# Top-32 attention before two dense layers on one core: early first products of chunk 0, values prepared in three steps, chunk 3 starting chunk 4, and x's two forms in one buffer

## The chip, the core and the metric

The program runs on one core of a Trainium2 chip. The metric is the device time of one execution in microseconds. The engines are PE (TensorE; PEld is its weight loads), DVE (VectorE), ACT (ScalarE), POOL (GpSimd) and SP, which issues the DMAs. Each takes its instructions in one fixed order.

## The reference

Attention for 4 batches of 8 heads, 576 rows of 64, in which each row keeps its 32 largest scores, and then two dense layers over the 2304 x 512 result (`scale` is 1/8):

```python
scores = scale * np.matmul(q, k.transpose(0, 1, 3, 2))
kth = np.partition(scores, -32, axis=-1)[..., -32:-31]
scores = np.where(scores >= kth, scores, -1000000000.0)
attn = softmax(scores)
x = np.matmul(attn, v)          # then heads side by side: 2304 x 512
x = (sigmoid(x @ w_gate) * (x @ w_val)) @ w_out      # 512 -> 1536 -> 512
x = np.maximum(x @ w_in, 0.0) ** 2 @ w_out2           # 512 -> 2048 -> 512
```

## The kernel before

The 2304 rows are 18 blocks of 128. `CHUNKS` groups them into 12 chunks: chunks 0 to 5 are one block each (N = 128), chunks 6 to 11 are two (N = 256). The attention of a chunk runs over four pairs of heads (`Pair`); a **unit** is one head and one block. A unit is scores on PE (`sp`), a copy to SBUF on ACT, seven ranking steps on DVE (`rank`: max, match_replace, max, ... so k = 0 to 6), the softmax on ACT and POOL, a transpose, and, once per pair, the product with the values (`xp`), copied by ACT into x of the chunk.

Chunks 0 and 1 (`PLAIN`) run their two layers in fp32 (`moe32`): products `pg` of six pairs of feature blocks (`fp`), tanh on ACT (`th`), the sum `acc1`, copied by ACT into `x_plain` again, then `ph` and `acc2`. While they run, ACT, DVE and POOL turn the weights, which arrive as 64-bit words, into fp32 (`conv`, ACT's lines L613 and L620). Later chunks use fp16 pairs (high and low part) in `moe`: `pg`, `pv` (layer 1), `acc1`, then `x2` with a common scale (a sum of squares by a product with ones, `x2pq`, and a maximum on DVE), then `ph`, `acc2`. `split_x` makes the two fp16 parts of x for chunks 2 to 5; ACT squares them first (`x_5pq` is the sum for chunk 5).

From chunk 4 on (`PRE0`), a chunk computes `NPRE` = 2 pairs of the next chunk's layer 1 ahead (`nxt`, into the tile `gp`), the first before its own last `acc1`, the others between `x2`'s squares and its second layer. Chunk 3 does not.

The attention of chunks 6 to 11 takes its values in fp16 pairs from DRAM. They are prepared once per batch and pair of heads, 12 times: `prep_values` loads the fp32 values (`vm`, `ve`), ACT squares them with a running sum (L204) and copies the sums to bf16 (L208); `split_values` sums over partitions on PE (`vn`, L217), DVE makes a power of two of it, ACT and POOL make the two parts (`vom`, `voe`; `vom` is in the tag `vo`, which has one buffer), and SP writes them out (`vd`).

Tiles of a tag share its buffers: `m4` has three of 4 KB per partition (x, its fp16 parts, `gp`, an early x2 and others), `acc` two PSUM banks, `wk` two, `tr` two.

The order on each engine is settled when the program is built: a scheduler takes the instructions by priority (`at`, `tc.high_priority`) and dependence. The main loop hands it attention units, weight steps and layer steps by due times `ta`, `tw`, `tm`; later, `lead` says how many units attention is ahead of the layers.

Of the kernel before, what the change touches and what calls it, by code (L numbers as in the profile page):

```python
# [21 lines left out]
P = 128  # L22
# [18 lines left out]
PRE0 = 4  # L41
# [6 lines left out]
SM2 = ()  # L48
# [18 lines left out]
KA = 7  # L67
GLATE = 30.0
EARLY = ("wg", "wv")
PB = 10  # L70

# [5 lines left out]
def tile_topk_attention__then__two_moe_layers(  # L77
# [111 lines left out]
    def prep_values(b, hp):  # L189
# [8 lines left out]
        for r in range(2):  # L198
            nc.sync.dma_start(ve[r * ST : (r + 1) * ST], src[:, SM:S].rearrange("h p d -> p h d"))
        om = apool.tile([P, 2, 2, CB, D], F16, tag="vo", bufs=1, name=f"vom_{n}")  # L200
        oe = apool.tile([P, 2, 2, D], F16, tag="we", bufs=3, name=f"voe_{n}")
        sm = apool.tile([P, 8], F32, tag="bs", bufs=3, name=f"vs_{n}")
        for x, (o, t) in enumerate(((om, vm), (oe, ve))):
            nc.scalar.activation(  # L204
                o[:, :, 0].bitcast(BF16), t, AF.Square, accum_out=sm[:, x : x + 1]
            )
        sb = sm.bitcast(BF16)[:, 4:6]
        nc.scalar.copy(sb, sm[:, 0:2])  # L208
        late_values.append((b, hp, n, vm, ve, om, oe, sm))

    late_values = []
# [77 lines left out]
    class Pair:  # L289
# [9 lines left out]
        def load(self):  # L299
            ci, hp = self.ci, self.hp  # L300
            for tt in self.tts:
                qn = apool.tile([P, 2, 2, D], F32, tag="qn", bufs=2, name=f"qn_{tt}_{hp}")
                for b, s0, o, n in pieces(tt):
                    for a in range(2):
                        nc.sync.dma_start(
                            qn[o : o + n, :, a, :],
                            q[b, 2 * hp : 2 * hp + 2, s0 : s0 + n].rearrange("h p d -> p h d"),
                        )
# [27 lines left out]
        def queries(self, tts):  # L336
            for tt in tts:
                qn = self.qt[tt]
                pt = ps_t.tile([P, 512], F32, tag="tr", name=f"qpt_{tt}_{self.hp}")
# [129 lines left out]
        def transpose(self, j, i, wk, dg):  # L469
# [7 lines left out]
            tp = ps_t.tile([P, 512], F32, tag="tr", name=f"tp_{tt}_{h}")  # L477
# [444 lines left out]
    def moe32(ci, xt):  # L922
# [4 lines left out]
        def l1_pair(fp):  # L927
            pg = ps_w.tile([P, 512], F32, tag="wk", name=f"pg_{ci}_{fp}")
            for t, name in enumerate(("wg", "wv")):
                for e in range(2):  # L930
                    for c in range(KM):
# [4 lines left out]
                            start=(t == 0 and e == 0 and c == 0),  # L936
                            stop=(c == KM - 1),
                            skip_group_check=True,
                        )
            th = mpool.tile([P, 2 * N], F32, tag="hi", bufs=HIB, name=f"th_{ci}_{fp}")  # L940
# [21 lines left out]

        prev = None
# [59 lines left out]
    done = set()  # L1023
    xsp = {}
# [6 lines left out]
    def attention():  # L1031
# [62 lines left out]
        def tail(n, after=None):  # L1094
# [30 lines left out]
            if j == 1 and i == len(pr.tts) - 1:  # L1125
                if pr.ci < TCI:
                    pr.values()
                if pr.hp == NHP - 1:
# [38 lines left out]
        for n in range(last + 1):  # L1167
# [8 lines left out]
            for u, k in orders(n):  # L1176
                if u in state:
# [9 lines left out]
                    seq.append(ins)  # L1187
            turns()
# [3 lines left out]
            while ci >= TCI - 2 and late_values:  # L1192
                split_values(*late_values.pop(0), seq[-1])
# [64 lines left out]
    for ci in PLAIN:  # L1258
        n = 0
        while True:  # L1260
            if nstep[0] == len(steps):
                tw = 1e8
            if body is None and ci in xsp:
                have("wv")
                body = moe32(ci, xsp.pop(ci))
# [88 lines left out]
```

## Time and profile before

| | |
|---|---|
| median of three runs | 1227.74 us (1220.72, 1227.74, 2309.37) |
| the profiled execution | 1218.28 us |
| its span, first to last instruction | 1216.2 us |
| PE busy, idle | 1158.1 us, 58.1 us |
| mean granted clock of PE | 0.989 |

The last of the three runs was disturbed as a whole; the other two and the profiled execution lie within 9.5 us. 2.08 us of the profiled execution lie outside its span.

### The profile page before, as it was taken

What the parts mean: (1) busy time and instruction counts of PE and PEld (TensorE: products, weight loads), DVE (VectorE), ACT (ScalarE), POOL (GpSimd) and SP (SyncE); (2) the same over time, 40 slices, a digit from 0 to 9 for tenths busy, and PEclk for the clock granted to TensorE, in tenths of its full rate; (3) what the DMA queues carried; (4) which work ended last, traced back from release to release, by engine and by line L of the source; (5) the groups of instructions that cost most, each with busy time, mean ns of one, the idle gap of its engine ahead of it and who ended that gap; (6) DMA issues with size and microseconds to landing.
All of it is one profiled execution on the core that took longest, in us unless ns stands there. A gap on an engine that the chain in (4) does not pass through costs nothing.

```text
span 1216.2 us, 30575 instructions
## 1 busy us (share of the span) xinstructions
PE 1158.1 (95%) x11477; PEld 941.4 (77%) x11477; DVE 919.5 (76%) x1921; ACT 802.0 (66%) x1695; POOL 833.4 (69%) x1294
## 2 busy tenths in 40 slices
PE   6879999999799799999999999999999999999998
PEld 5659878878679678788787688768876886886875
DVE  5899878899779988999999799999699969010010
ACT  3999985777767777777778667766577666222122
POOL 1698984687875688878879967896597659324223
PEclk9889999999899999999999999999999999999999
DMA  6999963324353477666676666556245513200000
GB/s 153 355 359 320 305 181 105 89 68 133 99 148 104 116 153 156 143 138 135 144 173 136 137 146 130 122 117 145 50 89 126 99 40 63 45 1 1 18 1 18
DMA packets 243187, 153.91 MB, mean 127 GB/s; under 512 B 193120, under 2 KB 209504, under 8 KB 243040
## 3 DMA queue, kind: packets, MB, share of 16 engines
q1 hardware_dynamic: 243040, 151.97, 49.3%
q8 instruction: 90, 1.47, 0.5%
q14 instruction: 57, 0.47, 0.1%
HBM read 105.51 MB, written 18.09 MB: 102 GB/s over the span
## 4 chain that ended last, share of the span: by engine, by line
PE 48%; DVE 2%; DMA 1%; SPq 0%; issue 0%; ACT 0%; POOL 0%; DVEq 0%; POOLq 0%
PE acc L899 10%; PE ph L878 10%; PE acc L813 7%; PE pv L773 7%; PE pg L773 7%; PE sp L381 3%; PE xp L516 3%; DVE mx L392 1%; DVE W L393 1%; PE qpt L341 1%; DMA kn<-in_k_dram 1%; DMA PT<-pp 0%; PE kpt L167 0%; PE x2pq L845 0%; DVE x2s L848 0%
## 5 line engine op out<-in xcount | busy, mean ns | idle before, releaser
L392 DVE MAX8 mx<-W 128x8 f32<-128x576 f32 x432 | 327.7, 759 | 10.9
L393 DVE MATCH_REPLACE8 W<-mx,W 128x576 f32<-128x576 f32 x288 | 213.9, 743 | 0.0
L878 PE MATMUL ph<-x,wi_w 128*128 128x256 f16 (+1 forms) x1920 | 191.8, 252 | 4.4 <-ACT r L887 2.8
L899 PE MATMUL acc<-w_w,rh 128*128 128x512 f16 x768 | 182.2, 379 | 1.6 <-POOL rh L891 1.6
L878 PEld LDWEIGHTS <-wi_w 128*128 128x128 f16 x1920 | 155.9, 98 | 30.7 <-issue 4.7
L773 PE MATMUL pg<-xs,wg_w 128*128 128x256 f16 (+1 forms) x1440 | 145.4, 251 | 1.3 <-ACT th L783 1.3
L773 PE MATMUL pv<-xs,wv_w 128*128 128x256 f16 (+1 forms) x1440 | 142.6, 251 | 2.1 <-DVE x2s L848 1.7
L381 PE MATMUL sp<-kst,qt 128*128 128x288 f32 x608 | 132.9, 328 | 9.4 <-DMA kst<-ks 4.7
L464 POOL TENSOR_TENSOR pp<-S,pp 128x512 f16<-128x512 f32 x192 | 137.1, 736 | 1.9
L773 PEld LDWEIGHTS <-wg_w 128*128 128x128 f16 x1440 | 117.2, 98 | 19.1 <-issue 3.4
L418 ACT ACTIVATE S<-S,mx 128x576 f32<-128x576 f32 x144 | 111.8, 776 | 27.7 <-DVE mx L392 27.3
L813 PEld LDWEIGHTS <-wo_w 128*128 128x128 f16 x1440 | 118.7, 99 | 13.9 <-issue 2.4
L899 PEld LDWEIGHTS <-rh 128*128 128x128 f16 x768 | 72.1, 98 | 73.4 <-POOL rh L891 1.8
L773 PEld LDWEIGHTS <-wv_w 128*128 128x128 f16 x1440 | 117.0, 98 | 15.4 <-issue 2.7
L392 DVE MAX8 mx<-S 128x8 f32<-128x576 f32 x144 | 107.2, 745 | 26.6 <-ACT S L384 26.4
L384 ACT COPY S<-sp 128x576 f32<-128x576 f32 x144 | 91.8, 637 | 50.6 <-PE sp L381 44.9
L785 DVE TENSOR_TENSOR th<-pv,th 128x512 f32<-128x512 f32 (+1 forms) x60 | 34.6, 576 | 119.2 <-PE pv L773 118.5
L462 POOL TENSOR_SCALAR S<-S,bs 128x576 f32<-128x576 f32 x96 | 71.9, 749 | 54.4 <-ACT pp L461 53.7
L393 DVE MATCH_REPLACE8 W<-mx,S 128x576 f32<-128x576 f32 x144 | 106.9, 743 | 0.0
L813 PE MATMUL acc<-gh,wo_w 128*128 128x256 f16 (+1 forms) x1104 | 104.9, 249 | 1.9 <-ACT gh L788 1.9
L381 PEld LDWEIGHTS sp<-kst,qt 128*128 128x128 f32 x608 | 90.2, 191 | 18.9 <-DMA kst<-ks 5.0
L890 POOL TENSOR_TENSOR r<-r 128x512 f32<-128x512 f32 (+1 forms) x80 | 69.5, 871 | 48.5 <-ACT rh L889 47.4
(236 smaller groups left out, 2222.2 us busy)
## 6 DMA issues: line engine op xcount, KB each, us to landing
kst<-ks SPq DMA_DIRECT2D x112, 288.0 KB, 3.1
v<-vd SPq DMA_DIRECT2D x32, 320.0 KB, 3.5
qn<-in_q_dram SPq DMA_DIRECT2D x128, 64.0 KB, 2.5
wi_r<-in_moe_w_in_dram SPq DMA_DIRECT2D x16, 512.0 KB, 6.4
w_r<-in_moe_w_out_dram SPq DMA_DIRECT2D x16, 512.0 KB, 4.9
v<-in_v_dram SPq DMA_DIRECT2D x56, 128.0 KB, 2.4
wg_r<-in_moe_w_gate_dram SPq DMA_DIRECT2D x12, 512.0 KB, 6.1
wv_r<-in_moe_w_val_dram SPq DMA_DIRECT2D x12, 512.0 KB, 7.3
```

What stands on the lines that cost most here:

```text
L381: nc.tensor.matmul(sp[:, e, 0:HALF], l, r, start=(x == 0), stop=(x == len(ops) - 1))
L384: nc.scalar.copy(ss.rearrange("p (e s) -> p e s", e=2), sp[:, :, 0:HALF])
L392: return nc.vector.max(m8, st.cur).ins
L393: ins = nc.vector.match_replace(st.wk, m8, st.cur, NEG).ins
L418: nc.scalar.activation(wk, wk, AF.Prelu, bias=kth, scale=-1.0, alpha=1.0 / BIG)
L462: nc.gpsimd.tensor_scalar(wk, wk, rz, 1.0, op0=ALU.mult, op1=ALU.mult)
L464: nc.gpsimd.tensor_tensor(pp[:, o : o + e - f], wk[:, f:e], pp[:, f:e], op=ALU.subtract)
L773: nc.tensor.matmul(pp[:, e * N : (e + 1) * N], wblk(wd, a, c, f0, P), xs[:, b_, c, :], start=(e == 0 and n == 0), stop=(n == 3 * KM - 1), ...
L813: nc.tensor.matmul(accs[d // 2][:, (d % 2) * N : (d % 2 + 1) * N], wblk("wo", a, f, d * P, P), gh[:, b_, e * N : (e + 1) * N], start=(f == ...
L878: nc.tensor.matmul(ph[:, e * N : (e + 1) * N], wblk("wi", a, c, f0, P), x2[:, b_, c, :], start=(e == 0 and n == 0), stop=(n == 3 * KM - 1) ...
L890: nc.gpsimd.tensor_tensor(r, r, r, op=ALU.mult)
L899: nc.tensor.matmul(acc2[i][:, 0:DM], gh[:, b_, e * N + i * P : e * N + (i + 1) * P], wblk("w2", a, f, 0, DM), start=(f == 0 and x == 0), s ...
```

## The change

- `products` takes the columns (`cs`) of x that a step works on. For chunk 0, once three of its four pairs of heads are in x, a first step of `moe32` issues the products of `FIRST` = 2 pairs `fp` with the first `XC` = 3 quarters of x; `l1_pair` then adds the fourth quarter alone.
- `QACC` = 2: the query transposes of chunk 0's first two pairs of heads go to a bank of `acc`, not `tr`. (`SIDEQ` and `TACC` are 0 and do nothing.)
- `prep_values` loads only. The squares and the copy (`norm_values`) are issued in the ranking of a unit, after its step k = 4 (`KB`), and `split_values` after step k = 6 (`KC`). The sums `sm` get a buffer of their own; they used the softmax's tag `bs`.
- `PRE0` = 3: chunk 3 too computes two pairs of the next chunk's layer 1 ahead, and its attention lead is `LEAD2` = 14 units, not `LEAD` = 10.
- `SM2`: for chunks 2 to 5 the fp16 parts of x lie in the second half of x's own buffer, not in a second buffer of `m4`.

```diff
-PRE0 = 4
+PRE0 = 3
...
-SM2 = ()
+SM2 = (2, 3, 4, 5)
...
+QACC = 2
...
+KB = 4
+KC = 6
+FIRST = 2
+FUP = 0
+XC = 3
...
+        later.append((KB, norm_values, (b, hp, n, vm, ve)))
+
+    later = []
+
+    def norm_values(b, hp, n, vm, ve, after):
         om = apool.tile([P, 2, 2, CB, D], F16, tag="vo", bufs=1, name=f"vom_{n}")
         oe = apool.tile([P, 2, 2, D], F16, tag="we", bufs=3, name=f"voe_{n}")
-        sm = apool.tile([P, 8], F32, tag="bs", bufs=3, name=f"vs_{n}")
+        sm = apool.tile([P, 8], F32, tag="sm", bufs=1, name=f"vs_{n}")
         for x, (o, t) in enumerate(((om, vm), (oe, ve))):
-            nc.scalar.activation(
+            sq = nc.scalar.activation(
                 o[:, :, 0].bitcast(BF16), t, AF.Square, accum_out=sm[:, x : x + 1]
             )
+            tc.add_manual_dep(sq.ins, after.name, NOSYNC, reason="loaded by then")
         sb = sm.bitcast(BF16)[:, 4:6]
         nc.scalar.copy(sb, sm[:, 0:2])
-        late_values.append((b, hp, n, vm, ve, om, oe, sm))
-
-    late_values = []
+        later.append((KC, split_values, (b, hp, n, vm, ve, om, oe, sm)))
...
-                pt = ps_t.tile([P, 512], F32, tag="tr", name=f"qpt_{tt}_{self.hp}")
+                pool, tag = (ps_a, "acc") if self.ci == 0 and self.hp < QACC else (ps_t, "tr")
+                pt = pool.tile([P, 512], F32, tag=tag, name=f"qpt_{tt}_{self.hp}")
...
-        def l1_pair(fp):
-            pg = ps_w.tile([P, 512], F32, tag="wk", name=f"pg_{ci}_{fp}")
+        early = {}
+
+        def products(fp, cs):
+            fresh = fp not in early
+            if fresh:
+                early[fp] = ps_w.tile([P, 512], F32, tag="wk", name=f"pg_{ci}_{fp}")
+            pg = early[fp]
             for t, name in enumerate(("wg", "wv")):
                 for e in range(2):
-                    for c in range(KM):
+                    for c in cs:
...
-                            start=(t == 0 and e == 0 and c == 0),
+                            start=(fresh and t == 0 and e == 0 and c == cs[0]),
...
+        def l1_pair(fp):
+            products(fp, range(XC if fp in early else 0, KM))
+            pg = early.pop(fp)
...
+        if ci == PLAIN[0] and FIRST:
+            for fp in range(FIRST):
+                products(fp, range(XC))
+            yield
...
                     seq.append(ins)
+                    while later and later[0][0] == k:
+                        _, fn, args = later.pop(0)
+                        fn(*args, ins)
...
-            while ci >= TCI - 2 and late_values:
-                split_values(*late_values.pop(0), seq[-1])
...
+            if (
+                ci == PLAIN[0]
+                and FIRST
+                and body is None
+                and xdone.get(ci, 0) >= XC
+                and nstep[0] > NF1 // 2 + XC // 2
+            ):
+                body = moe32(ci, xts[ci])
+                at(max(ta, tw) - FUP)
+                next(body)
+                tm = 1e9
```

**How the order changes.** On PE, just after x of chunk 0 is complete (`tp_1_0` is a transpose for the next chunk, `pg_0_0` the first product pair, `x_plain` x, `wg_c`, `wv_c` the weights), before:

```order
L665 MATMUL wv_n_590<-wv_d_793,ones_86 128x128
L482 MATMUL tp_1_0_1079<-dg_1_0_1014,S_1_0_822 128x128 x4
L932 MATMUL pg_0_0_1040<-x_plain_335,wg_c1_280 128x128
L932 MATMUL pg_0_0_1040<-x_plain_335,wg_c0_209 128x128 x2
L932 MATMUL pg_0_0_1040<-x_plain_335,wg_c1_280 128x128 x2
L932 MATMUL pg_0_0_1040<-x_plain_335,wv_c0_524 128x128
L381 MATMUL sp_1_4_1163<-kst_1_4_0_1062,qt_1_2_0_1074 128x288
L932 MATMUL pg_0_0_1040<-x_plain_335,wv_c0_524 128x128
```

and now, one pair of heads earlier, right behind `tp_0_6`:

```order
L496 MATMUL tp_0_6_935<-dg_0_6_866,S_0_6_627 128x128 x4
L951 MATMUL pg_0_0_868<-x_plain_335,wg_c1_280 128x128
L951 MATMUL pg_0_0_868<-x_plain_335,wg_c0_209 128x128 x2
L951 MATMUL pg_0_0_868<-x_plain_335,wg_c1_280 128x128
L951 MATMUL pg_0_0_868<-x_plain_335,wv_c0_524 128x128 x2
L951 MATMUL pg_0_0_868<-x_plain_335,wv_c1_582 128x128
L951 MATMUL pg_0_0_868<-x_plain_335,wv_c0_524 128x128 x2
L951 MATMUL pg_0_0_868<-x_plain_335,wv_c1_582 128x128
L951 MATMUL pg_0_1_881<-x_plain_335,wg_c1_280 128x128
```

Of the 32 products of the pairs 0 and 1, 6 stood ahead of the last quarter of x before, and 24 do now; 8 are left for after it.

On ACT, where chunk 0's layer-1 sum is copied (`x_plain<-acc1_0`; `w2_c` are weight conversions), before:

```order
L485 COPY PT_1_6_1831<-tp_1_6_1832 128x512
L494 COPY PE_1_3_1838<-tq_1_6_1839 64x128
L613 ACTIVATE w2_c1_1562<-w2_r3_0_1536 128x512
L620 ACTIVATE w2_r3_0_1536<-w2_r3_0_1536 128x512
L972 COPY x_plain_335<-acc1_0_1208 128x512
L384 COPY S_2_2_1994<-sp_2_2_1995 128x576
```

and now:

```order
L447 ACTIVATE S_2_0_1754,bs_2_0_2032<-S_2_0_1754,bs_2_0_2032 128x576
L627 ACTIVATE w2_c1_1562<-w2_r3_0_1536 128x512
L634 ACTIVATE w2_r3_0_1536<-w2_r3_0_1536 128x512
L999 COPY x_plain_335<-acc1_0_1208 128x512
L499 COPY PT_1_6_1831<-tp_1_6_1832 128x512
L508 COPY PE_1_3_1838<-tq_1_6_1839 64x128
```

The copy stands behind the same four conversions of `w2`; it is ACT's row 236, and was 239.

On ACT in chunk 2, between the squares of the values of batch 1, pair 1 (`vom_1_1`) and the copy of their sums that PE's `vn` waits for (`vs_1_1`), before:

```order
L783 ACTIVATE th_2_3_3883<-pg_2_3_3833,x_2s_2810 128x256
L204 ACTIVATE vom_1_1_3506,vs_1_1_3508<-vm_1_1_3500 128x2x256
L434 ACTIVATE S_4_0_3281,bs_4_0_3607<-S_4_0_3281,bs_4_0_3607 128x576
L434 ACTIVATE S_4_1_3362,bs_4_1_3718<-S_4_1_3362,bs_4_1_3718 128x576
L675 ACTIVATE wi_w6_3348<-wi_c6_1383,wsmall_89 128x1024
L208 CAST vs_1_1_3508<-vs_1_1_3508 128x2
```

and now:

```order
L689 ACTIVATE w2_w3_3180<-w2_c3_1586,wsmall_89 128x1024
L797 ACTIVATE th_2_3_3881<-pg_2_3_3831,x_2s_2809 128x256
L217 ACTIVATE vom_1_1_3579,vs_1_1_3581<-vm_1_1_3499 128x2x256
L744 ACTIVATE xt_3_2885<-xt_3_2885,x_3s_3564 128x512
L222 CAST vs_1_1_3581<-vs_1_1_3581 128x2
```

Three instructions stood between the two, and one does now. Over the twelve batches and pairs there were 30 such instructions, and there are 19.

On PE, where chunk 3 goes from layer 1 to layer 2 (`x_5pq` sums chunk 5's squares, `ph_3_0` is the first product of layer 2), before:

```order
L725 LDWEIGHTS ones_86
L725 MATMUL x_5pq_6138<-xs_5_6136,ones_86 128x128
L341 MATMUL qpt_6_1_6264<-ident_81,qn_6_1_5877 128x128 x2
L878 LDWEIGHTS wi_w0_2928
L878 MATMUL ph_3_0_5571<-x2_3_5551,wi_w0_2928 128x128
```

and now (`pg_4_1`, `pv_4_1` are chunk 4's layer 1):

```order
L787 MATMUL pg_4_1_5871<-xt_4_3699,wg_w1_2457 128x128
L394 MATMUL sp_6_2_6259<-kst_6_2_1_5724,qt_6_1_1_6113 128x288 x3
L859 LDWEIGHTS ones_86
L859 MATMUL x2pq_3_5855<-x2_3_5854,ones_86 128x128
L859 LDWEIGHTS ones_86
L859 MATMUL x2pq_3_5855<-x2_3_5854,ones_86 128x128
L787 LDWEIGHTS wv_w0_2454
L787 MATMUL pv_4_1_5872<-xt_4_3699,wv_w0_2454 128x128
```

The products of chunk 4's first two pairs (96 of 128 columns) stand now ahead of `ph_3_0`, the last 24 of them behind `x2pq_3`; `x_5pq` stands ahead of both sums `x2pq_3`.

## Rows read from the trace of the kernel before

**Rows 1.** the page's first part: busy us, share of the span, instructions of each engine.
```profile
PE 1158.1 (95%) x11477; PEld 941.4 (77%) x11477; DVE 919.5 (76%) x1921; ACT 802.0 (66%) x1695; POOL 833.4 (69%) x1294
```

**Rows 2.** windows; length, busy (instructions) of PE, PEld, DVE, ACT, POOL, clock, DMA, GB/s.
```profile
0.00:90.00 90.00, 67.60 (x385) 51.08 (x386) 72.41 (x147) 68.47 (x141) 50.32 (x68) 0.89 0.87 291
90.00:150.00 60.00, 58.48 (x524) 53.76 (x525) 53.98 (x112) 59.25 (x124) 55.63 (x63) 1.00 0.92 312
150.00:300.00 150.00, 147.16 (x1330) 123.78 (x1329) 130.81 (x244) 110.32 (x217) 107.00 (x143) 1.00 0.42 120
300.00:345.00 45.00, 36.85 (x477) 32.45 (x474) 33.97 (x77) 32.56 (x81) 35.22 (x63) 0.92 0.36 99
...
405.00:425.00 20.00, 13.13 (x166) 10.61 (x164) 19.15 (x51) 16.52 (x41) 14.40 (x27) 1.00 0.37 88
...
770.00:1216.20 446.20, 439.81 (x3934) 341.05 (x3931) 241.21 (x492) 221.57 (x431) 258.67 (x377) 1.00 0.29 62
```

**Rows 3.** timeline of PE: start, us, what; in brackets idle before and its releaser.
```profile
89.90 1.13 PE L482 MATMUL tp<-dg,S 128*128 128x128 f32 x8 [1.86 <-ACT x_plain L551]
...
93.02 1.60 PE L932 MATMUL pg<-x_plain,wv_c 128*128 128x128 f32 x12
```

**Rows 4.** timeline of ACT where chunk 0's sum is copied.
```profile
146.00 0.59 ACT L972 COPY x_plain<-acc 128x512 f32<-128x512 f32 x1
```

**Rows 5.** timeline of PE in chunk 2.
```profile
305.50 0.19 PE L217 MATMUL vn<-vs,ones 128*128 128x1 bf16 x2 [1.24 <-ACT vs L208]
...
319.66 0.27 PE L813 MATMUL acc<-gh,wo_w 128*128 128x128 f16 x2 [1.92 <-ACT gh L788]
321.33 1.45 PE L381 MATMUL sp<-kst,qt 128*128 128x288 f32 x6 [1.40 <-DMA kst<-ks]
...
327.58 0.19 PE L217 MATMUL vn<-vs,ones 128*128 128x1 bf16 x2 [1.23 <-ACT vs L208]
```

**Rows 6.** windows of 3 us, PE alone; busy, granted clock, DMA share, GB/s.
```profile
318.00:321.00 3.00, 0.27 (x2) 1.00 0.51 146
321.00:324.00 3.00, 2.67 (x20) 0.63 0.79 199
324.00:327.00 3.00, 1.62 (x15) 0.80 0.45 168
327.00:330.00 3.00, 1.63 (x9) 0.77 0.00 0
330.00:333.00 3.00, 3.00 (x27) 0.66 0.37 106
```

**Rows 7.** timeline of ACT between a batch's squares and its bf16 copy.
```profile
302.09 0.63 ACT L204 ACTIVATE vom<-vm 128x512 bf16<-128x512 f32 x1 [2.20 <-DMA vd<-vom]
...
302.72 0.76 ACT L434 ACTIVATE S<-S,bs 128x576 f32<-128x576 f32 x1
...
304.24 1.13 ACT L675 ACTIVATE wi_w<-wi_c,wsmall 128x1024 f16<-128x1024 f32 x1
305.28 0.17 ACT L208 CAST vs<-vs 128x2 bf16<-128x2 f32 x1
```

**Rows 8.** timeline of PE where chunk 3 goes from layer 1 to layer 2.
```profile
411.47 0.38 PE L725 MATMUL x_5pq<-xs,ones 128*128 128x128 bf16 x4 [1.74 <-ACT xs L722]
...
418.72 1.50 PE L878 MATMUL ph<-x,wi_w 128*128 128x128 f16 x24 [2.79 <-ACT r L887]
...
423.36 2.55 PE L899 MATMUL acc<-w_w,rh 128*128 128x512 f16 x11 [1.58 <-POOL rh L891]
```

**Rows 9.** timeline of PE at the same place of chunk 4.
```profile
488.14 0.79 PE L381 MATMUL sp<-kst,qt 128*128 128x288 f32 x4 [0.36 <-DMA kst<-ks]
...
498.91 0.94 PE L516 MATMUL xp<-PT,v 128*64 128x128 f16 x27 [1.46 <-DMA PT<-pp]
```

**Rows 10.** the page's groups, two steps of the ranking on DVE.
```profile
L392 DVE MAX8 mx<-W 128x8 f32<-128x576 f32 x432 | 327.7, 759 | 10.9
L393 DVE MATCH_REPLACE8 W<-mx,W 128x576 f32<-128x576 f32 x288 | 213.9, 743 | 0.0
```

More of the change, by code (lines that the diff above doesn't have):

```diff
@@ L67 @@
 KA = 7
+SIDEQ = 0
+QACC = 2
+TACC = 0
 GLATE = 30.0
@@ L304, in load @@
                     for a in range(2):
-                        nc.sync.dma_start(
+                        (nc.scalar if ci == 0 and hp == 0 and a < SIDEQ else nc.sync).dma_start(
                             qn[o : o + n, :, a, :],
@@ L476, in transpose @@
             ptr = self.pt[j]
-            tp = ps_t.tile([P, 512], F32, tag="tr", name=f"tp_{tt}_{h}")
+            pool, tag = (ps_a, "acc") if self.ci == 0 and self.hp < TACC else (ps_t, "tr")
+            tp = pool.tile([P, 512], F32, tag=tag, name=f"tp_{tt}_{h}")
             for c in range(CB):
@@ L1023, in tile_topk_attention__then__two_moe_layers @@
     done = set()
+    xdone = {}
     xsp = {}
@@ L1127, in tail @@
                     pr.values()
+                    xdone[pr.ci] = pr.hp + 1
                 if pr.hp == NHP - 1:
@@ L1262, in tile_topk_attention__then__two_moe_layers @@
                 tw = 1e8
-            if body is None and ci in xsp:
+            if (
[9 more added lines that the diff above has]
+                tm = 1e9
+            if ci in xsp and (body is None or tm == 1e9):
                 have("wv")
-                body = moe32(ci, xsp.pop(ci))
+                x = xsp.pop(ci)
+                body = moe32(ci, x) if body is None else body
                 tm = max(ta, tw if tw < 1e8 else 0)
```

## The prediction

> **What bounds the kernel now.** I read the page's first part, then windows by stage, then the timelines of PE and ACT where PE stands still. PE is busy 1158.1 of 1216.2 us and no other engine is near that [rows 1]; from 770 us on it is busy 439.81 of 446.2 us with DVE at half [rows 2]. What the change touches lies ahead of that, and the order on PE is the same again from about chunk 8 on. So the time falls by what PE's idle time (58.1 us in all) and its slow clock lose, and by nothing else: no instruction of weight goes or comes. Where that idle time lies decides. In the first 90 us PE is idle 22.4 us, but it waits there for others. From 90 to 150 us PE is busy 58.48 us and ACT 59.25 of 60 [rows 2]: both are full, and ACT a little more so. From 150 to 300 us PE is alone (147.16 of 150). Then come two holes: 300 to 345 us, with 8.15 us idle, and 405 to 425 us, with 6.87 us [rows 2]. These two and the first stretch are where this change acts.
>
> **Early products of chunk 0.** 18 products of 128 columns move from behind the last quarter of x to ahead of it. In the trace a product is two records, and 12 records take 1.60 us [rows 3], so 18 take 18 x 2 x 0.133 = 4.8 us. PE has room for them ahead of 90 us, and waits 1.86 us just there [rows 3]. If PE alone set the pace from 90 to 150 us, all 4.8 us would be won. But chunk 0 cannot go on to its second layer before ACT has copied the sum, at 146.00 us [rows 4], and ACT runs through that stretch without a pause of its own. In the new order this copy stands behind the same conversions, three instructions earlier; 124 instructions fill 59.25 us [rows 2], 0.478 us each, so it comes 3 x 0.478 = 1.4 us earlier. After that PE holds the lead. I take 1.4 us; the bounds are 0 (ACT's other rows slip by as much) and 4.8 us. The bank change for two query transposes I cost at nothing: it lies in the first 90 us, where PE's idle 22.4 us cover it; without that cover it is a transpose or two.
>
> The Trainium skill (page "PSUM — Partial Sum Buffer", section "Engine vs sequencer instructions") says that ScalarE's queue is strictly first in, first out. It speaks against this part: the copy cannot pass the conversions ahead of it. By that rule the term is the 1.4 us, without it the 4.8 us; the trace shows ACT's rows only in their built order and has nothing that passes.
>
> **Values in three steps.** `vn` on PE waited twice for ACT's copy, 1.24 and 1.23 us [rows 5], of twelve times in all. The copy came 3.0 us after the square [rows 7], since two exponentials and a 1.13 us weight split stood between; one instruction stands there now. ACT itself stood 2.20 us before that square, until the single `vo` buffer had been written out [rows 7]; the squares now come later against that write. I take the two waits, 2.5 us, and nothing for ACT's stall, which other work of PE hides in part. Upwards the stall adds 2.2 us. Downwards: the square is now let go by ranking step 4 and `vn` by step 6, two steps of 0.759 and 0.743 us [rows 10] for squares and a copy that take about 1.5 us on ACT. If ACT is behind, `vn` waits each time, and the work queued behind it on PE with it: ten more waits of 1.24 us are 12.4 us lost. With one instruction between instead of three I take the near end, no new wait. The loads, the writes and their places on SP's queue stay near where they were; batches 2 and 3 are ready about one unit later, and are used more than ten units after that.
>
> **The clock behind the hole.** From 318 to 321 us PE is busy 0.27 us, and then the granted clock is 0.63, 0.80, 0.77 and 0.66 for four windows [rows 6], a mix of 2.4 and 1.2 GHz. What is missing from full clock, times the busy time, is 0.37 x 2.67 + 0.20 x 1.62 + 0.23 x 1.63 + 0.34 x 3.00 = 2.7 us. The hole itself is made by a wait for ACT (1.92 us) and one for a key load (1.40 us) [rows 5], which the change does not remove but which ACT, freed of its stall, may shorten. I take half, 1.4 us, between 0 and 2.7.
>
> **Chunk 3 starts chunk 4; one buffer for x.** Where chunk 3 changes layers, PE waits 1.74 us for chunk 5's squares, 2.79 us for ACT's relu and 1.58 us for POOL's square [rows 8], 6.11 us together, since nothing else is in its queue. Chunk 4, which already has the first pairs of its successor there, waits 0.36 and 1.46 us at the same place [rows 9], 1.82 us. The difference, 4.3 us, is what I take; the bounds are 0 and 6.1. The products of chunk 4 are not new, only earlier, and take buffers: `gp` takes the `m4` buffer that chunk 3's x leaves, which is free because x and its parts now share one; without that sharing it would have to wait for chunk 3's own parts. Four more units of attention ahead of chunk 3's layers cost nothing on PE if DVE keeps up; from 405 to 425 us it is busy 19.15 of 20 us [rows 2], so it cannot go faster, only be asked earlier.
>
> **Sum.** 1218.28 - 1.4 - 2.5 - 1.4 - 4.3 = 1208.7 us for an execution like the profiled one. Of the three undisturbed executions (1218.28, 1220.72, 1227.74) that one is the fastest and the middle one lies 2.4 us above it, so I expect a median of 1211 us. The median of the runs shown, 1227.74, is the slower of the two runs that count.
>
> **Rivals.**
> - *All holes close.* The early products count in full (4.8), PE's idle time from 300 to 345 us goes whole (8.15, the two `vn` waits in it), the clock stays up (2.7), and all of the 6.1 us at chunk 3: 21.8 us, so 1196.5 + 2.4 = 1199 us. For it: after a hole the clock falls, so one hole less pays twice. Against it: ACT at 59.25 of 60 us, and a key load among the waits.
> - *The waits only change place.* PE takes its queue in order; when one wait goes, the next engine is met a little later. DVE is nearly full around chunk 3, and chunk 4's products, done earlier, are missing later as cover. Then only the 1.4 us of the first stretch stay: 1216.9 + 2.4 = 1219 us.
> - *The wait for the copy multiplies.* `vn` waits for ACT all twelve times, as worked out above, +12.4 us, while the first stretch and chunk 3 still give 5.7 us: 1218.28 + 6.7 + 2.4 = 1227 us, slower than before. It decides from a mean of more than 0.6 us on each of the ten new waits. For it: the two ranking steps leave ACT 1.5 us and no more, where before it had most of a unit. Against it: in the trace ten of twelve did not wait, with more instructions between.
>
> The Trainium skill (page "Perfetto Trace Analysis", section "Identifying the Most-Contended Engine") says that the busy share of matmuls is no good measure of a full PE and that of weight loads is better. By it PE would have 23% to spare, as weight loads are busy 77% [rows 1], some 280 us, and the first rival would not be the end. From 770 us on, however, weight loads are busy 341.05 of 446.2 us, 76%, while PE hardly pauses and no other engine is full [rows 2]; here 77% is a full PE, and the measurement decides.
>
> **How the numbers follow.** The forecast has 0.50 (its own range 1204 to 1217), all holes close 0.17, change of place 0.20, multiplied waits 0.13. The range 1200 to 1226 leaves out the far halves of the first and the last rival, some 0.15. A measurement of this kernel can tell about 2% from no change, 24 us: below 1196 would be faster, above 1245 slower. Only the first rival comes near the one (0.11 with the spread of the runs), and only the last, with more than it counts, near the other (0.03); within is 0.86.
>
> **What would show it.** Right: the copy of chunk 0's sum between 143 and 146 us; no `vn` that waits over 0.5 us for ACT's copy; clock 1.00 around chunk 2's end; less than 2.5 us idle on PE where chunk 3 changes layers; PE's idle time near 49 us. Wrong: that copy near 141 us (PE set the pace), PE idle as before with other releasers (change of place), or a row of `vn` waits for ACT (the last rival). A new hole in chunks 4 to 6, where the order moves by up to three units, would also spoil the sum; no row shows one.

## The result, and the profile after

The changed kernel takes 1208.74 us (median of four runs, 1206.68 to 1212.53). The kernel before, run beside it, takes 1221.42 us (1220.72 to 1227.74; a fourth run, 2309.37 us, was disturbed as a whole and is left out). The ratio is 0.9895, with a 95% interval of 0.9872 to 0.9917: some 1%, 13 us. The profiled execution took 1212.53 us (span 1210.6); it is the slowest of the four, and that of before, at 1218.28 us, lies below every run beside the changed kernel. So the two traces differ by 5.75 us where the medians differ by 12.7, and a part is better sized by leaving it out than by comparing these two traces.

The page's first part, after, answers to [rows 1]:

```profile
PE 1158.6 (96%) x11477; PEld 942.8 (78%) x11477; DVE 919.1 (76%) x1921; ACT 802.8 (66%) x1695; POOL 833.5 (69%) x1294
```

PE's work is the same (1158.6 us), and its idle time fell from 58.1 to 1210.6 - 1158.6 = 52.0 us. The windows say where (columns as in [rows 2]):

```profile
300.00:345.00 45.00, 37.03 (x498) 33.15 (x496) 36.06 (x83) 31.82 (x75) 35.39 (x58) 0.92 0.45 125
...
405.00:425.00 20.00, 19.51 (x303) 17.93 (x302) 16.52 (x44) 13.90 (x34) 14.20 (x27) 1.00 0.24 59
425.00:510.00 85.00, 80.57 (x1109) 66.37 (x1106) 77.65 (x172) 64.73 (x159) 72.03 (x133) 1.00 0.69 156
```

From 405 to 425 us PE was idle 6.87 us before [rows 2] and is idle 0.49 us now. The hole from 300 to 345 us is as large as it was: 7.97 us against 8.15, at the same granted clock of 0.92. The timeline of PE in chunk 2 and where chunk 3 changes layers answers to [rows 5, 8]:

```profile
305.54 0.19 PE L229 MATMUL vn<-vs,ones 128*128 128x1 bf16 x2 [0.89 <-ACT vs L222]
...
316.16 1.29 PE L394 MATMUL sp<-kst,qt 128*128 128x288 f32 x6 [1.80 <-DMA kst<-ks]
...
325.58 1.39 PE L827 MATMUL acc<-gh,wo_w 128*128 128x128 f16 x22 [2.10 <-POOL gh L803]
...
328.62 0.27 PE L859 MATMUL x2pq<-x,ones 128*128 128x128 bf16 x2 [1.52 <-ACT x L857]
329.45 0.19 PE L229 MATMUL vn<-vs,ones 128*128 128x1 bf16 x2 [0.56 <-ACT vs L222]
...
410.84 0.39 PE L739 MATMUL x_5pq<-xt,ones 128*128 128x128 bf16 x4
...
415.11 1.50 PE L787 MATMUL pv<-xt,wv_w 128*128 128x128 f16 x24 [0.38 <-DVE x2s L862]
416.44 4.45 PE L892 MATMUL ph<-x,wi_w 128*128 128x128 f16 x72
```

In chunk 2 `vn` still waits twice for ACT's copy (0.89 and 0.56 us, before 1.24 and 1.23), and the hole is made of waits for a key load (1.80, before 1.40), for POOL's `gh` (2.10, before 1.92 for ACT's) and for ACT's x2 (1.52, before 0.73). At chunk 3's change of layers the three waits of [rows 8] are gone; the row ahead of `ph` has the only one left, 0.38 us. The timeline of ACT answers to [rows 4, 7]:

```profile
146.04 0.57 ACT L999 COPY x_plain<-acc 128x512 f32<-128x512 f32 x1
...
304.07 0.63 ACT L217 ACTIVATE vom<-vm 128x512 bf16<-128x512 f32 x1 [2.05 <-DMA vd<-vom]
...
327.57 0.63 ACT L217 ACTIVATE vom<-vm 128x512 bf16<-128x512 f32 x1 [0.80 <-DMA vd<-vom]
...
340.79 0.63 ACT L217 ACTIVATE vom<-vm 128x512 bf16<-128x512 f32 x1 [1.97 <-DMA vd<-vom]
```

The copy of chunk 0's sum comes at 146.04 us, before at 146.00. PE's last products of that sum, before and now, do move:

```profile
143.49 2.05 PE L954 MATMUL acc<-g,wo_c 128*128 128x128 f32 x16
```

```profile
141.78 2.05 PE L977 MATMUL acc<-g,wo_c 128*128 128x128 f32 x16
```

They end at 145.54 us before and at 143.83 now. The copy followed 0.46 us behind them, and now it follows 2.21 us behind, when ACT, which runs without a pause, comes to it. ACT's stall for the one `vo` buffer has not gone: 2.05, 0.80 and 1.97 us before the squares of batch 1's pairs 1 to 3, where the kernel before has 2.20, none and 1.21.

### The profile page after: what moved, and what is told of

Same layout as the page of the kernel before. It is cut to its first block, busy times and chain, and to the rows that moved or that the text cites. A ratio compares the mean times of both kernels' runs of the same rounds, so it can differ in the third digit from the quotient of the medians.

```text
span 1210.6 us, 30572 instructions
## 1 busy us (share of the span) xinstructions
PE 1158.6 (96%) x11477; PEld 942.8 (78%) x11477; DVE 919.1 (76%) x1921; ACT 802.8 (66%) x1695; POOL 833.5 (69%) x1294
## 4 chain that ended last, share of the span: by engine, by line
PE 47%; DVE 2%; DMA 2%; POOL 2%; ACT 1%; issue 1%; SPq 0%; POOLq 0%; DVEq 0%; ACTq 0%
PE ph L892 11%; PE acc L913 10%; PE acc L827 7%; PE pg L787 7%; PE pv L787 6%; PE sp L394 3%; PE xp L530 3%; DMA PT<-pp 1%; DVE W L406 1%; DVE mx L405 1%; PE qpt L354 1%; POOL pp L477 1%; DMA kst<-ks 1%; POOL S L475 0%; SPq L317 0%
## 5 line engine op out<-in xcount | busy, mean ns | idle before, releaser
L787 PE MATMUL pg<-xs,wg_w 128*128 128x256 f16 x864 | 106.2, 273 | 0.4 <-DVE th L799 0.4
L827 PE MATMUL acc<-gh,wo_w 128*128 128x256 f16 (+1 forms) x1056 | 102.2, 248 | 2.2 <-POOL gh L803 2.1
L787 PE MATMUL pv<-xs,wv_w 128*128 128x256 f16 x864 | 103.6, 273 | 0.5 <-DVE x2s L862 0.5
L474 ACT ACTIVATE pp<-S,bs 128x576 f16<-128x576 f32 x96 | 74.4, 775 | 43.6 <-issue 19.4
```

The lines of the kernel that those rows point to most:

```text
L474: nc.scalar.activation(pp[:, 0:S], wk, AF.Copy, scale=rz)
L787: nc.tensor.matmul(pp[:, e * N : (e + 1) * N], wblk(wd, a, c, f0, P), xs[:, b_, c, :], start=(e == 0 and n == 0), stop=(n == 3 * KM - 1), ...
L827: nc.tensor.matmul(accs[d // 2][:, (d % 2) * N : (d % 2 + 1) * N], wblk("wo", a, f, d * P, P), gh[:, b_, e * N : (e + 1) * N], start=(f == ...
```

## The experiments

Each kernel was timed in five rounds beside the kernel before, on the same chip (11 to 29 runs of it in a job, medians of 1220.73 to 1222.99 us). Ratios are to that kernel, with 95% intervals; those of the experiments are ±0.0015 to ±0.0027, so 0.1 points (0.001 of the ratio) are 1.2 us, and two ratios differ clearly only from some 0.3 points on. "Chunk 3's start" is short for `PRE0 = 3`, "the steps" for the values in three steps. The early products always go with their bank change (`QACC`), and the steps with the own buffer of `sm`; no run separates these pairs, so what is said of a part holds for the pair.

### One part alone

**Chunk 3's start alone**, on the kernel before:

```diff
-PRE0 = 4
+PRE0 = 3
```

> The kernel before, with PRE0 = 3 alone: chunk 3 computes two pairs of chunk 4 ahead, everything else as before. Theory 1 (the sum as predicted, term by term): 4.3 us faster than before, ratio 0.9965, and the idle time of 6.1 us on PE at chunk 3's change of layers falls to about 2 us. Theory 2 (this part carries the whole gain, since in the changed kernel's profile PE is 3.4 us later than before at the start of chunk 2's second layer and 9.4 us earlier at the start of chunk 4's): 11 to 13 us faster, ratio 0.990. Rival (the buffer of m4 that x's parts shared is needed for gp): with two buffers per x, gp waits for chunk 3's parts, and less than 3 us are gained.

Measured: 1249.43 us, ratio 1.0227 (1.0202 to 1.0253), 28 us slower, where all three forecasts had a gain. The rival named the right buffer, but it is chunk 5's parts that wait for `gp`, and not `gp` for chunk 3's. The timeline of its engines from chunk 3 to chunk 4, `gp` being chunk 4's early products and `xs` the parts of chunk 5's x:

```profile
450.95 0.94 PE L823 MATMUL acc<-gp,wo_w 128*128 128x128 f16 x14
...
453.63 0.39 PE L735 MATMUL x_5pq<-xs,ones 128*128 128x128 bf16 x4
...
452.04 0.62 ACT L732 ACTIVATE xs<-xt 128x512 bf16<-128x512 f32 x1
...
447.44 0.42 DVE L795 TENSOR_TENSOR th<-pv,th 128x256 f32<-128x256 f32 x1 [26.52 <-POOL th L794]
```

ACT can start `xs` of chunk 5 at 452.04 us, when PE has read `gp` for the last time (450.95 + 0.94 us): `gp` has the `m4` buffer that `xs` needs. The sum `x_5pq` comes at 453.63 us instead of 411.47 [rows 8]. On DVE the next ranking step stands behind the scale made from it, and that behind `th` of chunk 4's layer 1: DVE is idle 26.52 us in one piece before that `th`, and ranks again from 456 us on. The windows show who pays:

```profile
425.00:510.00 85.00, 80.93 (x1083) 67.43 (x1080) 50.07 (x117) 47.35 (x113) 59.20 (x105) 0.98 0.40 86
510.00:770.00 260.00, 234.51 (x2437) 189.66 (x2437) 241.95 (x517) 188.34 (x415) 202.00 (x350) 0.94 0.67 148
```

DVE is busy 50.07 of 85 us, and later PE is idle 25.5 of 260 us at a clock of 0.94.

**Early products alone**, on the kernel before (with the code of `products` as in the change):

```diff
+QACC = 2
+FIRST = 2
+XC = 3
```

> The kernel before, with the early products of chunk 0 alone (FIRST = 2, XC = 3, QACC = 2). Theory 1 (ACT sets the pace of the first 150 us; three instructions less ahead of the copy): 1.4 us faster, ratio 0.999. Theory 2 (ACT sets the pace and the copy of chunk 0's sum comes no earlier, as in the changed kernel's profile, 146.04 against 146.00 us): 0 us. Rival (PE sets the pace): 4.8 us faster, ratio 0.996, with the copy near 141 us.

Measured: 1226.55 us, ratio 1.0041 (1.0026 to 1.0055): slower, by 5 us, which none of the three forecasts had. And yet chunk 0's sum is copied at 143.51 us, and chunk 1's layer 2 starts at 238.65 us, before at 241.43. The lead is lost at the end of chunk 2, as POOL and PE show there (L234 and L235 are the split of the values, L457 the softmax's scaling of `S`):

```profile
323.60 0.71 POOL L234 TENSOR_SCALAR vm<-vm,vsc 128x512 f32<-128x512 f32 x1
324.27 0.37 POOL L234 TENSOR_SCALAR ve<-ve,vsc 64x128 f32<-64x128 f32 x1
...
325.33 1.15 POOL L235 TENSOR_TENSOR vom<-vm,vom 128x512 f16<-128x512 f32 x1
326.44 1.41 POOL L235 TENSOR_TENSOR voe<-ve,voe 64x128 f16<-64x128 f32 x1
...
328.13 0.68 POOL L457 TENSOR_SCALAR S<-S,bs 128x512 f32<-128x512 f32 x1
...
328.87 2.07 PE L494 MATMUL tp<-ident,S 128*128 128x128 f32 x8 [4.02 <-POOL S L457]
```

PE's transposes wait 4.02 us for `S`, and ahead of `S` on POOL stand the four large rows of the split, 0.71 + 0.37 + 1.15 + 1.41 = 3.64 us. Layer 2 of chunk 2 starts at 330.73 us, before at 330.06: the lead is gone. Most of the 5 us of loss comes later: layer 2 of chunk 5 starts at 560.16 us, before at 555.36. No run shows what makes it.

**The steps alone**, on the kernel before (`prep_values`, `norm_values` and `split_values` as in the change):

```diff
+KB = 4
+KC = 6
...
+                    while later and later[0][0] == k:
+                        _, fn, args = later.pop(0)
+                        fn(*args, ins)
...
-            while ci >= TCI - 2 and late_values:
-                split_values(*late_values.pop(0), seq[-1])
```

> The kernel before, with the values prepared in three steps alone. Theory 1: 2.5 to 3.9 us faster (the two waits of vn, and half of the clock's loss), ratio 0.997 to 0.998. Theory 2 (the waits only change place: in the changed kernel's profile PE's idle time from 300 to 345 us is 7.97 us against 8.15, vn waits 0.89 and 0.56 us, ACT still stands 2.05 us for the write of the vo buffer): within 1.5 us of before.

Measured: 1222.72 us, ratio 1.0001 (0.9985 to 1.0018): nothing, as Theory 2 has it. Of the waits of `vn` in chunk 2 one is left, 1.77 us at 340.48 us, beside a wait of 2.45 us for ACT's `gh`. The window from 405 to 425 us is the last row:

```profile
304.28 0.27 PE L827 MATMUL acc<-gh,wo_w 128*128 128x128 f16 x2 [2.45 <-ACT gh L802]
...
340.48 0.19 PE L229 MATMUL vn<-vs,ones 128*128 128x1 bf16 x2 [1.77 <-ACT vs L222]
...
405.00:425.00 20.00, 17.99 (x234) 15.94 (x232) 17.64 (x46) 14.19 (x34) 13.83 (x25) 0.91 0.37 87
```

PE is idle only 2.01 us there, before 6.87, and still nothing is won: idle time that goes from one window is not yet time won.

**The shared buffer alone**, on the kernel before:

```diff
-SM2 = ()
+SM2 = (2, 3, 4, 5)
```

> The kernel before, with x and its two parts in one buffer for chunks 2 to 5 alone. All theories but one: within 2 us of before, since nothing waits for a buffer of m4 in the rows read. Rival (the m4 buffers held back chunk 4's and chunk 5's x): 3 to 6 us faster, and the wait of 1.74 us for chunk 5's squares is gone.

Measured: 1222.33 us, ratio 1.0009 (0.9992 to 1.0025): nothing, as nobody asks for the buffer that it frees.

So no part gains anything alone, two of them lose, and together they gain 1%. What follows takes parts from the whole.

### Parts together

**Chunk 3's start with the shared buffer**, without early products and steps:

```diff
-PRE0 = 4
+PRE0 = 3
...
-SM2 = ()
+SM2 = (2, 3, 4, 5)
```

> The kernel before, with PRE0 = 3 and the shared buffer of x, without early products and with the old preparation of the values. Theory 1 (the two belong together: alone, PRE0 = 3 puts gp into the buffer that chunk 5's parts wait for, and x_5pq comes at 453.6 instead of 411.5 us): x_5pq near 410 us, 10 to 14 us faster than before, ratio 0.989 to 0.992. Rival (the early products or the values are needed too): less than 6 us faster.

Measured: 1228.62 us, ratio 1.0050 (1.0029 to 1.0070). The buffer takes back 22 of the 28 us: `x_5pq` comes at 416.57 us. But a loss of 6 us stays, where Theory 1 had a gain of 10 to 14. Its timeline where chunk 3 changes layers (SPq is SP's queue, L862 the scaled copy of x2, L212 the squares of the values):

```profile
417.41 0.91 SPq L204 DMA_DIRECT2D vm<-in_v_dram  x2
...
418.14 0.78 ACT L427 ACTIVATE S<-S,mx 128x576 f32<-128x576 f32 x1 [0.28 <-DVE x2s L143]
421.23 0.63 ACT L212 ACTIVATE vom<-vm 128x512 bf16<-128x512 f32 x1 [2.31 <-DMA ke<-in_k_dram]
421.86 0.82 ACT L862 ACTIVATE x<-acc,x2s 128x256 f16<-128x256 f32 x2
...
422.36 2.91 PE L888 MATMUL ph<-x,wi_w 128*128 128x128 f16 x29 [2.97 <-ACT x L862]
```

The loads of the values of batch 2, pair 1 are issued at 417.41 us, two in a row, and land about 3.1 us after their issue (the median of the two), so the second at some 421 us. Their square stands on ACT ahead of x2's copy and holds it for 2.31 us (the load named as releaser, `ke`, is the next one on the same queue). `ph`, which needs x2, starts after a wait of 2.97 us.

**The whole without the early products:**

```diff
-QACC = 2
+QACC = 0
...
-FIRST = 2
+FIRST = 0
```

> The changed kernel, without the early products of chunk 0 (FIRST = 0, QACC = 0). Theory 1 (alone the early products made the kernel 0.4% slower, and they do so here too): 3 to 7 us faster than the changed kernel's 1208.7, ratio to before 0.984 to 0.987. Rival A (they gain where the rest is changed): 3 to 5 us slower than the changed kernel, ratio 0.992 to 0.994. Rival B (what they cost alone is only another order by chance): within 2 us of the changed kernel.

Measured: 1214.04 us, ratio 0.9928 (0.9904 to 0.9952). The early products, which lose 0.4 points alone, are worth 0.33 points, some 4 us, when the rest is there; that is Rival A's number, at the edge of the noise. The steps, the only difference to the kernel with 1.0050, bring 1.2 points.

**The whole without the steps** (values prepared as before):

```diff
-        later.append((KB, norm_values, (b, hp, n, vm, ve)))
...
+        late_values.append((b, hp, n, vm, ve, om, oe, sm))
...
+            while ci >= TCI - 2 and late_values:
+                split_values(*late_values.pop(0), seq[-1])
```

> The changed kernel, with the old preparation of the values. Theory 1 (the three steps do nothing, as alone): within 2.5 us of the changed kernel, ratio to before 0.987 to 0.992. Rival (the old squares stand in ACT's queue where chunk 3 changes layers, and cost there as the order is now): 4 to 8 us slower, ratio 0.993 to 0.997.

Measured: 1222.22 us, ratio 0.9999 (0.9982 to 1.0016): without the steps nothing of the whole gain is left, more than the 4 to 8 us of the rival. PE and POOL at the end of its chunk 2:

```profile
328.58 1.16 POOL L235 TENSOR_TENSOR vom<-vm,vom 128x512 f16<-128x512 f32 x1
...
331.64 0.69 POOL L457 TENSOR_SCALAR S<-S,bs 128x512 f32<-128x512 f32 x1
...
332.39 1.85 PE L494 MATMUL tp<-ident,S 128*128 128x128 f32 x7 [3.21 <-POOL S L457]
```

It is the place of the early products alone: `tp` waits 3.21 us for `S`, which comes from POOL behind the split's L235 rows. Yet against the kernel with chunk 3's start and the buffer (1.0050) the early products gain 0.51 points here: this wait does not decide whether they gain.

**The whole without chunk 3's start** (its lead is 10 units again with it):

```diff
-PRE0 = 3
+PRE0 = 4
```

> The whole change except that chunk 3 does not start chunk 4 (its attention lead is 10 units again). Theory (the gain is made where chunk 3 changes layers, and the buffer and the three steps only make that possible): nearly nothing is left, a ratio to the kernel before of 0.998 to 1.005, PE idle again 4 us or more from 405 to 425 us, and layer 2 of chunk 4 starts near 487 us or later. Rival (the values in three steps or the early products bring gains of their own once together): 0.993 to 0.997, although the hole from 405 to 425 us is back.

Measured: 1216.23 us, ratio 0.9951 (0.9935 to 0.9967). This is the rival's number: early products and steps, of which one loses and the other brings nothing alone, gain 0.5 points together, without chunk 3 (the shared buffer, nothing alone, is in this kernel too). What the steps change for the early products is on POOL and PE at the end of chunk 2 (L239 is of the split, L461 the scaling of `S`):

```profile
319.28 1.65 POOL L461 TENSOR_SCALAR S<-S,bs 128x512 f32<-128x512 f32 x1 [0.78 <-DVE bs L452]
...
330.43 1.15 POOL L239 TENSOR_TENSOR vom<-vm,vom 128x512 f16<-128x512 f32 x1
...
325.60 0.66 PE L498 MATMUL tp<-ident,S 128*128 128x128 f32 x4
...
409.74 5.55 PE L892 MATMUL ph<-x,wi_w 128*128 128x128 f16 x72 [1.48 <-ACT x L866]
...
405.00:425.00 20.00, 17.47 (x203) 14.23 (x199) 18.07 (x49) 14.74 (x35) 16.86 (x30) 0.91 0.50 114
```

The scaling of `S` now stands at 319.28 us, 11 us ahead of this row of the split, and `tp` (325.60 us) does not wait. Layer 2 of chunk 2 starts at 328.25 us, 2.5 us sooner than with the early products alone. The ratio there is 0.9 points (11 us) higher, so most of the difference comes later: layer 2 of chunk 6 starts at 641.70 us here and at 652.18 there, and no row was tied to that. The `ph` row is chunk 3's change of layers, where PE waits 1.48 us for x2's copy; from 405 to 425 us PE is idle 2.53 us, less than the 4 us that the theory gave and than the 6.87 us before, though chunk 3 has no products of chunk 4.

**Chunk 3's start, the shared buffer, and one of the twelve batches and pairs in steps**, no early products; the other eleven are prepared in the old way (for the one, the split too moves behind step k = 6):

```diff
+        if (b, hp) == (2, 1):
+            later.append((KB, norm_values, (b, hp, n, vm, ve)))
+        else:
+            norm_values(b, hp, n, vm, ve, None)
```

> Chunk 3 starts chunk 4 and x has one buffer, no early products; the values are prepared in the old way, except for batch 2, pair 1, whose squares go through the three steps: with that they no longer stand ahead of the scaled copy of x2 of chunk 3 on ACT, where they waited 2.31 us for their load. Theory (that one stall at the change of layers is what the three steps take away): 0.993 to 0.999 where the old way in all twelve gave 1.005, layer 2 of chunk 3 starts 2 to 4 us sooner than the 422.4 us there, and PE is idle under 1.5 us from 405 to 425 us. Rival (the steps help a little at many of the twelve places): 1.001 to 1.006, with the idle time of chunk 3 gone but given back in chunks 4 to 6.

Measured: 1218.17 us, ratio 0.9963 (0.9944 to 0.9981), against 1.0050 with none and 0.9928 with all twelve in steps: one of twelve brings 0.87 of the 1.22 points. Its timeline at the place of the 2.31 us:

```profile
416.95 0.78 ACT L440 ACTIVATE S<-S,mx 128x576 f32<-128x576 f32 x1 [0.27 <-DVE mx L414]
417.63 0.82 ACT L875 ACTIVATE x<-acc,x2s 128x256 f16<-128x256 f32 x2
...
418.14 4.36 PE L901 MATMUL ph<-x,wi_w 128*128 128x128 f16 x72
```

x2's copy stands right behind the softmax row, and `ph` starts with no wait in its row, at 418.14 us and not 422.36. The theory holds for this place. But 4.2 us are less than half of the 0.87 points (10.6 us): by layer 2 of chunk 4 the two traces are 6.3 us apart (485.79 and 492.07 us), and no row shows where the rest comes from. The other 0.35 points lie somewhere in the other eleven.

**The lead of chunk 3**, in the changed kernel:

```diff
-        lead = LEAD if ci < PRE0 else LEAD2
+        lead = LEAD if ci < 4 else LEAD2
```

> The changed kernel, but the attention runs only 10 units ahead of the layers of chunk 3, as before, not 14. Theory (chunk 4's products are what fills PE at chunk 3's change of layers, and the four more units only go beside them): the ratio to the kernel before stays near that of the changed kernel, 0.987 to 0.992, and PE is idle under 1.5 us where chunk 3 changes layers. Rival (with chunk 4's products done earlier, those units of attention are the cover that is missing later): 0.993 to 0.999, chunk 3's change of layers is still closed, but PE waits 3 us or more in addition in the second half of chunk 3 and in chunk 4, from 425 to 510 us.

Measured: 1210.97 us, ratio 0.9915 (0.9895 to 0.9935), not to be told from the changed kernel. Its windows:

```profile
405.00:425.00 20.00, 20.00 (x297) 17.60 (x294) 16.39 (x43) 13.86 (x33) 15.77 (x29) 1.00 0.32 75
425.00:510.00 85.00, 78.95 (x1060) 65.12 (x1057) 74.92 (x168) 63.04 (x155) 69.90 (x130) 0.98 0.70 152
```

Chunk 3's change of layers is closed without the four units too (20.00 of 20 us), and from 425 to 510 us PE is idle 6.05 us, 1.6 more than in the changed kernel and not the 3 that the rival gave. The kernel without chunk 3's start (0.9951) has the same lead of ten, so this pair prices chunk 3's start by itself: 0.36 points, 4.4 us.

### Who sets the pace of the first chunk

The same two kernels, with and without early products, while the low words of the weights are left out:

```diff
-            for e, r in enumerate(rs):
-                low = r[:, :, 0].bitcast(I32)
-                nc.scalar.activation(low, r[:, :, 0], AF.Copy, scale=float(2.0**-29))
-                nc.gpsimd.tensor_tensor(
-                    c.bitcast(I32)[:, e], c.bitcast(I32)[:, e], low, op=ALU.add
-                )
```

> The changed kernel, but the low words of the weights are left out: for each weight block ACT's conversion of the low word and POOL's addition of it fall away, so the outputs come from weights cut to their high words. ACT and POOL have less to do from 20 to 300 us. Theory (ACT sets the pace of the first chunk, so the early products bring 2.6 us there, not 4.8): the copy of chunk 0's sum comes 4 us or more sooner than in the same kernel without early products, and sooner than 140 us. Rival (PE's own order, or the arrival of the weights, sets the pace): the two copies lie 2 to 3 us apart as with the low words, and not far from 145 us.

> The same without the low words of the weights and without the early products. Theory (ACT sets the pace): its copy of chunk 0's sum comes 4 us or more later than with the early products, and sooner than the 147.1 us that the kernel with low words has. Rival: 2 to 3 us later than with them.

Measured: with early products 1201.21 us, ratio 0.9810 (0.9784 to 0.9837), without them 1203.09 us, ratio 0.9830 (0.9806 to 0.9854); 0.2 points, within the intervals. The copy of chunk 0's sum and the window from 90 to 150 us, with early products:

```profile
134.99 0.58 ACT L993 COPY x_plain<-acc 128x512 f32<-128x512 f32 x1
```

```profile
90.00:150.00 60.00, 59.14 (x568) 54.71 (x567) 56.94 (x129) 43.42 (x92) 15.83 (x37) 1.00 0.92 316
```

and without:

```profile
138.28 0.57 ACT L993 COPY x_plain<-acc 128x512 f32<-128x512 f32 x1
```

```profile
90.00:150.00 60.00, 58.43 (x559) 53.27 (x558) 56.64 (x126) 43.24 (x93) 15.22 (x38) 1.00 0.94 334
```

With ACT at 43 of 60 us and POOL at 15 to 16, both copies come some 9 us sooner than with the low words (147.4 and 144.6 us in the mean, below), so these conversions do set the pace there; which of the two engines, this cannot tell, since both were freed. But the two copies are 3.29 us apart, neither the 4 us of the theory nor clearly more than with the low words. That the two are no further apart has its reason on PE: without the low words its last product of the sum ends at 134.82 us with early products and at 137.68 without, 2.9 us apart and not 4.8, and the copy follows after 0.17 and 0.61 us. Why PE gains less there is not shown.

With the low words the traces do show ACT as the limit. Without early products (seven traces) PE's last product of the sum ends at 147.0 us in the mean, and the copy follows after 0.46 to 0.47 us; with them (five) it ends at 142.1, and the copy follows only after 2.21 to 2.59 us. PE wins 4.9 us, the whole 4.8 of the prediction's upper bound, and some 2 of them are lost in ACT's queue.

None of the kernels that compute the whole is faster than the changed one.

## Why the prediction came out right, and where its steps were wrong

The median (1208.74 us) lies 2.3 us under the forecast of 1211, and "within 2%" is what happened. The sum was right; its split was not, and neither was the form of a sum. That the total came out is in part luck: the term of 2.5 us for the steps rests on a wait that shrank by 1.0 us only, and other waits stood in for it. In us, where 0.1 points are 1.2 us:

| part | predicted | by leaving it out of the whole | alone, on the kernel before |
|---|---|---|---|
| early products | -1.4 (0 to -4.8) | -4.0 | +5.0 |
| values in three steps, with the clock | -2.5 - 1.4 | -12.7 | +0.1 |
| chunk 3 starts chunk 4 | -4.3 (0 to -6.1) | -6.8 (-4.4 at equal lead) | +28 (+6 with the buffer) |

The third column adds up to 23.5 us for a change of 13: each part's worth hangs on the others. All eight combinations are on record (chunk 3's start always with the buffer):

| | without chunk 3's start | with it |
|---|---|---|
| neither | 1.0000 | 1.0050 |
| early products | 1.0041 | 0.9999 |
| steps | 1.0001 | 0.9928 |
| both | 0.9951 | 0.9895 |

Early products lose 0.4 points alone and gain 0.3 to 0.5 beside either other part or both. Each part alone brings nothing or a loss, and each pair does better than either of its parts.

- **Early products.** The place and the limit, ACT's queue, were right and the size too small. Seven traces without them (the kernel before and six experiments, those without low words left out) have the copy of chunk 0's sum at 146.00 to 148.20 us, 147.4 in the mean; five with them, the changed kernel among these, at 143.51 to 146.04, 144.6 in the mean. That is 2.8 us, between the 1.4 us taken and the 4.8 us above: PE's sum is ready 4.9 us sooner, and ACT, which the prediction saw as the limit, gives some 2 back. The changed kernel's own trace (146.04) happens to be the latest of its five and the trace before (146.00) the earliest of its seven, so this pair shows nothing. Left out of the sum, and wrongly, was what an earlier chunk 0 meets later: at the end of chunk 2 the split on POOL, 3.64 us, ahead of the softmax, and more in chunks 3 to 5 that no row explains.
- **Values in three steps.** This step failed. It counted `vn`'s two waits for ACT's copy, 2.5 us; they fell by (1.24 + 1.23) - (0.89 + 0.56) = 1.0 us. (By [rows 7] the copy starts 3.2 us after the square's start, not 3.0; no term hangs on it.) What the steps bring lies in two places that it did not look at: a square that waits for its load no longer stands on ACT ahead of x2's copy of chunk 3 (0.87 points when it alone is moved), and in the kernels with early products the split no longer stands on POOL ahead of `S`. The first is shown by an experiment of its own; for the second there are the rows of five kernels (two with the wait and the split ahead, three with neither), and no run that moves this alone. It is small: layer 2 of chunk 2 starts at 330.73 and 334.25 us in the two, at 328.25, 330.18 and 333.43 in the three. ACT's stall for `vo`, which I left at nothing, did not shrink (4.82 us in all, before 3.41).
- **The clock behind the hole.** Not there: the hole stayed, and the granted clock from 300 to 345 us is 0.92 as before. Other kernels with the steps had 0.96 (the lead of ten) and 1.00 (without chunk 3's start) in the same window, so it can rise, but it did not make this result.
- **Chunk 3's change of layers.** Right in its place and its condition, and about right in its size: 4.4 us at equal lead and 6.8 us with the four more units, some 3 us either way, for the 4.3 taken. The reading behind it, that PE's idle time in this place is the price, is not borne out. From 405 to 425 us it fell by 6.4 us, to 0.49, but 4.3 of these are gone without chunk 3's start too (2.53 us left), and with the steps alone 4.9 are, with no time won. The condition (the shared buffer, "without that sharing it would have to wait") is worth 22 of 28 us, though what has to wait is chunk 5's parts, for `gp`. The second condition, that no square waits for its load in that place, was not in the prediction. That four more units of lead cost nothing held (0.9915 without them, 0.9895 with them, within the intervals).
- **The rivals.** The waits did change place in chunk 2, as the second rival had it, but only there. `vn` waits twice of twelve times as before, so the third rival did not begin.
- **What would show it.** Right: PE's idle time at chunk 3, and the copy between 143 and 146 us for the mean of five traces; the changed kernel's own, at 146.04, is just outside. Wrong: two waits of `vn` over 0.5 us, and the clock around chunk 2's end. PE's idle time is 52.0 us, not 49.

The Trainium skill (page "PSUM — Partial Sum Buffer", section "Engine vs sequencer instructions") has ScalarE's and GpSimd's queues strictly first in, first out. The traces agree: with 2.31 us to wait for a square's load, ACT did nothing of the x2 copy behind it, and POOL scaled `S` only after 3.64 us of split. In the prediction this rule was held against the early products alone, and it bore on the steps.

Left open: where the other 0.35 points of the steps come from, and all that the two places named do not account for; why the early products meet the split at the end of chunk 2 and the kernel before does not, and why they lose alone and gain beside either other part; and how much of chunk 3's start is the hole, of which 2.0 us of idle time go with it, and how much comes later. A second buffer for `vo`, which might take ACT's 2 us stalls away, was not tried.

## What to carry to other kernels

When a step is moved, look at what it stood in front of on each engine that takes its queue in order, not only at who waits for its result: here one square that waited 2.3 us for its load on ACT, moved by itself, took 10.6 us off a kernel, while the result itself had been late by 1.2 us. Parts that fill the same hole or share buffers need not have prices of their own; leave each out of the whole before adding prices up or dropping the part that loses alone, and do not take idle time gone from one window for time won. And where a kernel's start varies by 2 us from trace to trace, one pair of traces cannot size a gain of 2 to 3 us; the same row of many kernels with and without the part can.

## What was not expected of the hardware

The granted clock of PE between 60 and 70 us differs between kernels with and without the early products, at the same busy share of the engine. Two windows of the whole without early products:

```profile
40.00:50.00 10.00, 9.81 (x45) 7.90 (x46) 8.74 (x18) 8.34 (x18) 8.30 (x9) 0.51 1.01 377
...
60.00:70.00 10.00, 7.88 (x46) 5.78 (x45) 9.88 (x24) 10.00 (x22) 9.15 (x10) 0.70 1.05 379
```

and of the changed kernel, with the first of its early products that were moved:

```profile
40.00:50.00 10.00, 7.62 (x38) 5.96 (x38) 7.35 (x15) 9.03 (x18) 6.32 (x9) 1.00 1.00 370
...
60.00:70.00 10.00, 7.92 (x74) 5.96 (x72) 8.40 (x20) 9.93 (x21) 9.26 (x9) 1.00 1.04 375
...
72.90 1.06 PE L951 MATMUL pg<-x_plain,wg_c 128*128 128x128 f32 x8
```

PE is busy 7.88 and 7.92 of 10 us, and the clock is 0.70 (a mix of the two levels, 1.2 and 2.4 GHz) against 1.00. In all seven traces without early products it lies between 0.66 and 0.73 in this window, in all five with them it is 1.00. But the moved products cannot be what raises it: they start at 72.90 us here, and at 70.98 us or later in all five, behind the window, and in the two traces shown the clock is apart (0.51 and 1.00) from 40 to 50 us already. What comes with them and acts earlier is the bank change of the query transposes (the second of these runs at 14.12 us instead of 16.62); no run has it alone, so the cause is open. Without the low words of the weights the clock was 0.66 with early products too. Nor does this clock set the copy of chunk 0's sum: with the early products alone it was 0.74 from 30 to 60 us, and the copy came earliest of all, at 143.51 us.
